# Spreading the high and low part steps of a pair over several attention steps on VectorE, and moving the sum of v away from the rows

## The chip, the cores and the metric

The kernel runs on one core of one Trainium2 chip. The metric is the device time of one execution in microseconds (us), as the median of several executions. Executions of one kernel scatter here by 0.3 to 1.4% (lowest to highest), so kernels are compared by runs taken in turn with the kernel before on the same chip.

Engines are named as in the profile: PE is TensorE (matmul), PEld its weight loads, DVE is VectorE, ACT is ScalarE, POOL is GpSimd, SP is SyncE, which here only issues DMA (SPq in the views is its queue). PSUM is the memory into which PE writes; an eviction is an instruction of another engine that reads a result out of it, and the program lets a PSUM tile be written again only when it has been read. "L200" is line 200 of the kernel; `hT<-g,f` means that tile hT is written from tiles g and f.

## The reference, cut to what matters

Attention with a mask by cluster, then a gated feed-forward network.

```python
B, H, S, D = 4, 8, 768, 64                     # 16 clusters per head
q_assign = argmax(q_n @ c_n.T);  k_assign = argmax(k_n @ c_n.T)   # normalised
mask = q_assign[..., :, None] == k_assign[..., None, :]
attn = softmax(where(mask, q @ k.T / 8, -1e9)) @ v
x = attn.transpose(0, 2, 1, 3).reshape(B * S, H * D)              # 3072 x 512
out = (sigmoid(x @ w_gate) * (x @ w_val)) @ w_out                 # d_ff 1536
```

## The kernel before

The kernel works in 16-bit floats. To keep the choice of cluster exact, every q and k value, scaled by 64, is split into a high part h (rounded to 16 bits) and a low part l (the remainder); h and l lie side by side, are transposed together, and go through the matmul as a contraction of 128. In the later batches a DMA does the transpose. The mask is added by "rows": one-hot vectors of the clusters, transposed, which are written over the low parts.

PE runs attention of one block of tokens and, interleaved piece by piece, the feed-forward network of the block before, first its input phase (`ffn_in`), then its output phase (`ffn_out`). A block of a later batch has 24 attention steps (4 head pairs x 6 key chunks) and a batch has 48 steps. A plan says in which step each side job is put into the program; the order of the program is the order of each engine's queue.

```python
natp = ctx.enter_context(tc.tile_pool(name="nat", bufs=8))
op_ = ctx.enter_context(tc.tile_pool(name="o", bufs=2))          # output tiles
fp_ = ctx.enter_context(tc.tile_pool(name="f", bufs=3, space=bass.MemoryType.PSUM))
avp = ctx.enter_context(tc.tile_pool(name="av", bufs=1, space=bass.MemoryType.PSUM))
...
def split_h(b, pr, side, eng=None):
    hl = HL[b, pr, side] = hlp.tile([128, 2 * NCH, 2, D], HP, name="hl")
    ...
    nc.vector.tensor_scalar(hl[:, :, 0, :], nat, SC, None, ALU.mult)          # L195
def split_l(b, pr, side):
    nc.vector.scalar_tensor_tensor(                                           # L200
        hl[:, :, 1, :], nat, SC, hl[:, :, 0, :], ALU.mult, ALU.subtract)
def split(b, pr, side, eng=None):
    split_h(b, pr, side, eng); split_l(b, pr, side)
...
def rows(b, pr):
    po = fp_.tile(...)                     # six PE transposes into it: L278
    nc.vector.tensor_scalar(ohc, po[:, 0:S], OHV, None, ALU.mult)             # L284
    ...                                    # four DMAs from SP: L287
def mean_v(b, hs):
    sp = fp_.tile([128, 512], FP, name="f")
    nc.tensor.matmul(out=sp[:, 0:n], lhsT=ones, rhs=VS[b][...], ...)          # L403
    nc.vector.tensor_scalar(SV[b][...], sp[:, 0:n], EPS, None, ALU.mult)      # L410
...
def ffn_in(b, c0, n):
    for fc in range(NFC):
        for i in range(2):                 # gate, value: 4 matmuls each, L531
            gv.append(fp_.tile([128, 512], FP, name="f"))
            ...
            nc.scalar.activation(g[:, 0:w], gv[0][:, 0:w], AF.Tanh, scale=0.5)  # L540
        nc.vector.scalar_tensor_tensor(hT[:, fc, 0:w], g, 1.0, gv[1], ...)      # L542
def ffn_out(b, c0, n):
    ...                                    # 12 matmuls of 512 columns, L552
        osb = op_.tile([128, DM], FP, name="osb")
        nc.scalar.activation(osb, o, AF.Copy, scale=0.5)                      # L561
        nc.sync.dma_start(out=dst[:, c0 + t, :], in_=osb)                     # L562
...
def by_dma(b, pr, load, a, base):          # pair pr of batch b; a is a step of batch base
    at(base, load, load_pair, b, pr)
    for i, side in enumerate((1, 0)):      # keys, then queries
        at(base, a + 0.5 * i, split, b, pr, side)
        at(base, a + 0.5 * i, trans_dma, b, pr, side)
        at(base, a + 9 + i, classify, b, pr, side)
    at(base, a + 11.5, rows, b, pr)
...
by_dma(1, 2, E + 23, E + 36, 0)            # E = 8
by_dma(1, 3, E + 33, E + 43, 0)
for b in range(2, B):
    for pr in range(NPR):
        by_dma(b, pr, 10 * pr, 8 + 10 * pr, b - 1)
```

The other lines that matter: L460 adds the matmul result of a pair (`avs<-av,sv`, DVE), L470 multiplies it on POOL (`x<-avs,ri`), L490 are the score matmuls, L499 the exponentials on ACT (`es`), L450 the matmuls with v (`av`), L75 the loads of q and k, L232 and L511 transposing DMAs.

The softmax here doesn't subtract the row's maximum and nothing guards it: scores larger than these inputs give would overflow.

## Time and profile before

| | before |
|---|---|
| median of 4 runs | 365.25 us (364.83 to 366.24) |
| span in the profile, granted clock | 363.4 us, 0.993 |
| PE / ACT / DVE busy | 344.6 / 244.6 / 169.5 us |

First the page of the kernel before: the span, the engines' busy time with its share of the span, and the shares of the chain of work that ended last.

```profile
span 363.4 us, 9364 instructions
...
PE 344.6 (95%) x3887; PEld 228.1 (63%) x3887; DVE 169.5 (47%) x374; ACT 244.6 (67%) x359; POOL 71.5 (20%) x105
...
PE 78%; DMA 6%; DVE 5%; issue 5%; ACT 4%; SPq 1%; POOL 0%; ACTq 0%; DVEq 0%
```

PE bounds the kernel, but busy time flatters it, because pipelined matmuls overlap in the record (one of 384 columns lasts about 0.32 us there, and the next starts after 0.162). So I use one measure throughout, worked out from the trace: the time between the starts of two consecutive matmuls, less the usual spacing after a matmul of that shape (162 ns for 384 columns, 215 for 512, 29 for 65, 25 for 16). I call the rest a *loss* and count those over 60 ns. An ordinary hand-over, as to or from the transposes of the rows, costs about 0.1 us. From 104 to 260 us the kernel before loses 8.8 us, and from 270 us to the end almost nothing.

What PE waited for, in the view of waits (us in total, times, longest):

```profile
PE f L403 <- DVE ohc L284: 1.7, 2, 1.0
PE f L278 <- ACT g L540: 1.5, 2, 0.8
PE sc L490 <- ACT es L499: 1.4, 3, 0.8
...
PE f L531 <- DVE hT L542: 1.3, 5, 0.4
...
PE av L450 <- DVE avs L460: 0.7, 3, 0.4
```

One such place in the timeline (start, duration, engine, line, what; in brackets the idle time before it and what ended it), the fourth pair of a batch:

```profile
156.57 0.55 DVE L195 TENSOR_SCALAR hl<-nat 128x768 f16<-128x768 f32 x1
...
157.15 0.96 DVE L200 SCALAR_TENSOR_TENSOR hl<-nat,hl 128x768 f16<-128x768 f32 x1
...
158.03 0.55 DVE L542 SCALAR_TENSOR_TENSOR hT<-g,f 128x384 f16<-128x384 f32 x1
...
158.49 0.72 DVE L195 TENSOR_SCALAR hl<-nat 128x768 f16<-128x768 f32 x1
...
158.63 0.49 PE L278 MATMUL f<-ident,ohw 128*64 128x128 f16 x6 [0.76 <-ACT g L540]
...
159.25 0.96 DVE L200 SCALAR_TENSOR_TENSOR hl<-nat,hl 128x768 f16<-128x768 f32 x1
...
160.12 0.54 DVE L284 TENSOR_SCALAR ohc<-f 64x768 f16<-64x768 f16 x1
...
160.72 0.28 PE L403 MATMUL f<-vs,ones 128*128 128x260 f16 x1 [0.67 <-DVE ohc L284]
```

DVE does h, l, an hT, h, l without a break; what comes behind them in its queue (hT, ohc) is late, and PE stands twice. (The first wait is put down to g of L540; that g and the late hT both end at 158.58.) In the view by windows (busy us of each engine in a stretch) the two stretches of this kind show it too:

```profile
150.00:166.00 16.00, 14.57 (x177) 9.72 (x176) 9.14 (x19) 10.49 (x16) 3.00 (x4) 1.00 0.65 171
...
232.00:248.00 16.00, 14.24 (x175) 9.53 (x174) 9.39 (x18) 10.16 (x15) 2.85 (x4) 1.00 0.71 168
```

The columns are PE, PEld, DVE, ACT and POOL, then the granted clock, the DMA share and GB/s. PE stands 1.4 and 1.8 us of 16, while DVE is busy for only 9 of them: not too much work, but work in one lump.

### The profile page before, as it was taken

The numbers are of one execution on the slowest core, as the hardware profiler recorded it, in microseconds if no ns is written. First come the engines' busy times: TensorE is split into PE (matmuls) and PEld (weight loads), VectorE is DVE, ScalarE is ACT, GpSimd is POOL, SyncE is SP. The second block draws the span as 40 slices with busy tenths as digits, with TensorE's granted clock in tenths as the row PEclk, the third lists the DMA queues.
The fourth block names the chain that finished last, engine by engine and source line by source line (L and its number), as shares of the span: only waits on it lengthen the run. The fifth ranks groups of instructions, "written<-read, shape, count | busy, mean of one in ns | idle before, by whom it ended". The sixth has DMA issues, their size and how long they took to land.

```text
span 363.4 us, 9364 instructions
## 1 busy us (share of the span) xinstructions
PE 344.6 (95%) x3887; PEld 228.1 (63%) x3887; DVE 169.5 (47%) x374; ACT 244.6 (67%) x359; POOL 71.5 (20%) x105
## 2 busy tenths in 40 slices
PE   8699999999989999989999999989999999999995
PEld 4597877876566656656556656656556656664652
DVE  4678686647164725373344725373313322331330
ACT  6687698686577575857577574857578867881421
POOL 3720021436010120425010120425000000000000
PEclk9989999999999999999999999999999999999999
DMA  8999279466629363760619373761310031003002
GB/s 258 338 203 191 66 223 185 128 142 89 154 95 248 71 168 89 200 160 12 164 67 261 30 199 86 236 112 27 73 74 2 0 74 58 2 2 101 32 0 87
DMA packets 67466, 42.72 MB, mean 118 GB/s; under 512 B 45568, under 2 KB 64352, under 8 KB 67424
## 3 DMA queue, kind: packets, MB, share of 16 engines
q1 hardware_dynamic: 61488, 37.38, 40.0%
q0 software_dynamic: 5792, 4.72, 8.3%
q8 instruction: 30, 0.49, 0.5%
q14 instruction: 12, 0.10, 0.1%
q10 hardware_dynamic: 144, 0.03, 0.0%
HBM read 28.61 MB, written 6.29 MB: 96 GB/s over the span
## 4 chain that ended last, share of the span: by engine, by line
PE 78%; DMA 6%; DVE 5%; issue 5%; ACT 4%; SPq 1%; POOL 0%; ACTq 0%; DVEq 0%
PE f L531 30%; PE f L552 16%; PE sc L490 15%; PE av L450 8%; PE f L243 4%; DMA vn<-in_v_dram 3%; ACT es L499 2%; PE f L216 2%; DVE hl L195 1%; DMA out_dram<-osb 1%; PE f L278 1%; DVE hT L542 1%; DMA nat<-in_q_dram 1%; DMA nat<-in_k_dram 1%; PE f L295 1%
## 5 line engine op out<-in xcount | busy, mean ns | idle before, releaser
L499 ACT ACTIVATE es<-sc,nbias 128x768 f16<-128x768 f32 (+1 forms) x200 | 173.6, 877 | 71.1 <-PE sc L490 66.2
L542 DVE SCALAR_TENSOR_TENSOR hT<-g,f 128x384 f16<-128x384 f32 (+1 forms) x96 | 51.1, 534 | 84.0 <-PE f L531 46.4
L450 PEld LDWEIGHTS <-es 128*128 128x128 f16 x1152 | 59.8, 97 | 27.1 <-issue 3.7
L470 POOL TENSOR_TENSOR x<-avs,ri 128x384 f16<-128x384 f32 (+1 forms) x32 | 26.8, 837 | 245.5 <-DVE ri L469 196.6
L450 PE MATMUL av<-va,es 128*128 128x65 f16 x1152 | 67.5, 194 | 1.3 <-DVE avs L460 0.7
L540 ACT ACTIVATE g<-f 128x384 f32<-128x384 f32 (+2 forms) x108 | 48.8, 452 | 18.6 <-PE f L531 9.7
L552 PE MATMUL f<-wo_194,hT 128*128 128x512 f16 x138 | 38.3, 379 | 0.0
L552 PE MATMUL f<-wo_193,hT 128*128 128x512 f16 x138 | 38.1, 379 | 0.0
L460 DVE TENSOR_TENSOR avs<-av,sv 128x390 f32<-128x390 f32 (+2 forms) x36 | 18.6, 516 | 41.0 <-PE av L450 40.4
L552 PEld LDWEIGHTS <-hT 128*128 128x128 f16 x276 | 24.4, 97 | 21.1
L200 DVE SCALAR_TENSOR_TENSOR hl<-nat,hl 128x768 f16<-128x768 f32 x32 | 32.6, 1017 | 0.8
L260 DVE TENSOR_REDUCE mx<-f 128x12 f32<-128x192 f32 x32 | 11.4, 356 | 32.3 <-PE f L243 32.2
L561 ACT ACTIVATE osb<-f 128x512 f32<-128x512 f32 x24 | 14.2, 593 | 17.6 <-PE f L552 15.3
L531 PE MATMUL f<-xT,w_186 128*128 128x384 f16 (+2 forms) x108 | 25.6, 308 | 0.0
L531 PE MATMUL f<-xT,w_187 128*128 128x384 f16 (+2 forms) x108 | 25.6, 307 | 0.0
L531 PE MATMUL f<-xT,w_188 128*128 128x384 f16 (+2 forms) x108 | 24.1, 307 | 0.4 <-DVE hT L542 0.4
L531 PE MATMUL f<-xT,w_191 128*128 128x384 f16 (+2 forms) x108 | 24.0, 307 | 0.5 <-ACT g L540 0.5
L531 PE MATMUL f<-xT,w_189 128*128 128x384 f16 (+2 forms) x108 | 23.8, 307 | 0.5 <-DVE hT L542 0.5
L531 PE MATMUL f<-xT,w_192 128*128 128x384 f16 (+2 forms) x108 | 23.6, 307 | 0.4 <-DVE hT L542 0.4
L531 PE MATMUL f<-xT,w_190 128*128 128x384 f16 (+2 forms) x108 | 23.8, 307 | 0.0
L531 PE MATMUL f<-xT,w_185 128*128 128x384 f16 (+2 forms) x108 | 23.6, 308 | 0.2
L370 POOL CAST va<-vn 128x768 f16<-128x768 f32 x15 | 14.2, 951 | 10.6 <-DMA vn<-in_v_dram 10.6
(221 smaller groups left out, 449.1 us busy)
## 6 DMA issues: line engine op xcount, KB each, us to landing
nat<-in_k_dram SPq DMA_DIRECT2D x16, 384.0 KB, 3.9
vn<-in_v_dram SPq DMA_DIRECT2D x8, 768.0 KB, 6.8
nat<-in_q_dram SPq DMA_DIRECT2D x16, 384.0 KB, 4.8
out_dram<-osb SPq DMA_DIRECT2D x24, 256.0 KB, 2.1
wo_193<-in_moe_w_out_dram POOLq DMA_DIRECT2D x1, 768.0 KB, 17.1
wo_194<-in_moe_w_out_dram POOLq DMA_DIRECT2D x1, 768.0 KB, 12.2
w_185<-in_moe_w_gate_dram POOLq DMA_DIRECT2D x1, 384.0 KB, 7.8
w_189<-in_moe_w_val_dram POOLq DMA_DIRECT2D x1, 384.0 KB, 8.0
```

Source lines behind the costliest of these rows:

```text
L200: nc.vector.scalar_tensor_tensor(hl[:, :, 1, :], nat, SC, hl[:, :, 0, :], ALU.mult, ALU.subtract)
L243: nc.tensor.matmul(out=cl[:, o : o + NCL], lhsT=T[b, pr, side][:, hh, bass.ts(c, 128)], rhs=cT[:, r, bass.ts(2 * pr + hh, NCL)], start=(r ...
L370: nc.gpsimd.tensor_copy(va[:, :, :, 0:D], src)
L450: nc.tensor.matmul(out=av[:, o : o + D + 1], lhsT=es[:, hh, bass.ts(g * n + t, 128)], rhs=VA[b, pr][:, hh, j0 + g, :], start=(j0 + g == 0 ...
L460: nc.vector.tensor_tensor(s[:, :, 0:n, :], av[:, 0 : 2 * n * (D + 1)].rearrange("p (h t d) -> p h t d", h=2, t=n), SV[b][:, 2 * pr : 2 * p ...
L470: (nc.vector if n == 1 else nc.gpsimd).tensor_tensor(x[:, 0:n, 2 * pr * D : 2 * (pr + 1) * D].rearrange("p t (h d) -> p h t d", h=2), s[:, ...
L490: nc.tensor.matmul(out=sc[:, hh, g * n * 128 : (g + 1) * n * 128], lhsT=T[b, pr, 1][0 : D + NCL, hh, bass.ts(j0 + g, 128)], rhs=rhs, start ...
L499: nc.scalar.activation(es[:, :, 0:w], sc[:, :, 0:w], AF.Exp, bias=nbias, scale=es_scale)
L531: nc.tensor.matmul(out=gv[i][:, 0:w], lhsT=wgv[i][fc * NQ // NFC][:, dc, bass.ts(fc % (NFC // NQ), 128)], rhs=xT[:, 0:n, dc, :], start=(dc ...
L540: nc.scalar.activation(g[:, 0:w], gv[0][:, 0:w], AF.Tanh, scale=0.5)
L542: nc.vector.scalar_tensor_tensor(hT[:, fc, 0:w], g[:, 0:w], 1.0, gv[1][:, 0:w], ALU.add, ALU.mult)
L552: nc.tensor.matmul(out=o, lhsT=hT[:, fc, bass.ts(t, 128)], rhs=wo[fc * 2 // NFC][:, fc % (NFC // 2), :], start=(fc == 0), stop=(fc == NFC ...
```

## The change

The intent is to break up that lump: h of the keys at step a, l at a+1, h of the queries at a+2, l at a+3. And the sum of v (mean_v) of the first four heads leaves the step next to the rows, which take a PSUM tile of the same pool.

```diff
     def by_dma(b, pr, load, a, base):
         at(base, load, load_pair, b, pr)
         for i, side in enumerate((1, 0)):
-            at(base, a + 0.5 * i, split, b, pr, side)
-            at(base, a + 0.5 * i, trans_dma, b, pr, side)
+            at(base, a + 2 * i, split_h, b, pr, side)
+            at(base, a + 2 * i + 1, split_l, b, pr, side)
+            at(base, a + 2 * i + 1, trans_dma, b, pr, side)
...
-        at(b - 1, e + 40, mean_v, b, range(0, H // 2))
+        at(b - 1, e + 44, mean_v, b, range(0, H // 2))
```

## The prediction

> **What bounds the kernel.** TensorE. The page gives PE 344.6 us of a 363.4 us span (95%), ACT 67%, DVE 47%. The Trainium skill ("Perfetto Trace Analysis", Identifying the Most-Contended Engine) warns that matmul busy time is a poor measure, so I compared starts of consecutive matmuls in the trace with their steady spacing (162 ns for 384 columns, 215 for 512, 29 for 65). From 90 us on PE issues back to back: stretches such as 130:140 or 210:220 lose 0.1 us in 10. What is lost, about 10 us between 90 and 330, comes in a few clusters, and nothing later makes it good.
>
> **Where they lie.** Every pair of a later batch puts h, l, h, l (L195 0.55 us, L200 0.96 us) on DVE within one attention step (about 1.4 us), so DVE is taken for 3.0 to 3.5 us, and the hidden-layer evictions (hT, L542) and sums (avs) queue behind. In the timeline and the waits: after the splits at 105.5/187.5 PE loses 0.68 us (ACT g, then hT); at 121.8/203.8 1.1 us (g, hT, avs); at 156.6/238.6 0.9 us, followed by 0.83/1.16 us where the matmul of mean_v (L403) waits for the eviction of the rows (ohc), issued half a step before it. At 76 to 87 us about 1.4 us (avs, hT). The splits at 140/222 fall in the output-projection phase and cost nothing. Sum: about 8.8 us, the most the change can win.
>
> **The change.** No instruction is added or removed. h and l of the keys go to steps a, a+1, of the queries to a+2, a+3; each transposing DMA follows its l. mean_v of the first four heads moves four steps later, away from the rows. In the input phase an hT falls due every 2.04 us or so (8 matmuls at 2.7 per half step). One l and one hT take 1.5 us, h, l and hT 2.06 us, so DVE keeps pace, and the three PSUM buffers hide the rest. Transposes start up to 3.5 us later, but are needed seven to nine steps later: no cost.
>
> **What stays.** The second pair's l at a+3 now meets POOL's casts of v, which follow its x product; L200 took 1.46 instead of 0.96 us in this trace each time such a POOL instruction ran beside it. That fits the Trainium skill ("SBUF — State Buffer", SBUF: two separate sides): the shared ports are an exclusive lock. There the two onehots, ohc and avs also fall among the four steps, so I expect about 0.5 us to stay per batch; about 0.3 at the fourth pair, and half of the loss before 90 us. The first pair's l leaves the x product and should be 0.96.
>
> **Estimate.** Recovered: 0.7 before 90 us; per batch 0.6 + 0.6 + 1.5, twice: about 6 us; less a discount for stalls that only move: 5.2 us. Predicted 360.2 us, 8 in 10 between 357.8 and 363.2. Faster by over 2% (below 358.1): 0.12; within 2%: 0.86; slower: 0.02.
>
> **What would show it.** PE's waits on hT, g and avs near those splits, and on ohc at L403, shrink to tenths; PE's busy sum unchanged, span shorter by the idle time. No 1.46 us L200 in the first pair, perhaps one in the second. DVE's busy sum the same. The last 100 us unchanged in length.
>
> **What would make it wrong.** The gaps are set by f-buffer rotation (classify, rows, mean_v each take one of three), so that single l steps still stall PE; mean_v, now behind the second sum_v in the program, waits for it; later transposes hold up loads or stores in SP's order; the part before 90 us is ordered by the framework and may fall out otherwise; the 1.3 us stall at 102 to 103 us (ACT waits for an output DMA) may grow or vanish.

## The result, and the profile after

Ratios here are the mean time of one kernel's fast runs over that of the kernel before's fast runs of the same rounds, so they are not quite the ratio of the medians.

| | before | after |
|---|---|---|
| median of 4 runs | 365.25 us | 360.81 us (360.29 to 362.46) |
| ratio | | 0.9882 (0.9843 to 0.9921) |
| span in the profile, granted clock | 363.4 us, 0.993 | 360.7 us, 0.975 |

The kernel gained 4.4 us, or 1.2%: inside the range, close to the 5.2 us forecast. The profiled run was the slowest of the four. First its page:

```profile
span 360.7 us, 9360 instructions
...
PE 346.0 (96%) x3887; PEld 230.2 (64%) x3887; DVE 170.2 (47%) x374; ACT 244.9 (68%) x359; POOL 73.8 (20%) x105
...
PE 85%; DMA 6%; ACT 3%; SPq 2%; issue 1%; DVE 1%; POOL 0%; ACTq 0%
```

DVE went from 5% to 1% of the chain. From the same matmul (the 601st of L531) to the end it is 89.1 us before and after: the last part kept its length, as predicted. The waits of PE after the change:

```profile
PE sc L490 <- ACT es L499: 2.2, 2, 2.0
...
PE f L531 <- ACT g L540: 0.5, 1, 0.5
...
PE av L450 <- DVE avs L460: 0.2, 1, 0.2
```

The waits on hT and ohc are gone, those on g and avs almost, but one wait on `es` has become 2.0 us long. First the place that was shown above, the fourth pair:

```profile
159.06 0.55 DVE L195 TENSOR_SCALAR hl<-nat 128x768 f16<-128x768 f32 x1
...
159.53 0.55 DVE L542 SCALAR_TENSOR_TENSOR hT<-g,f 128x384 f16<-128x384 f32 x1
...
160.00 1.11 DVE L200 SCALAR_TENSOR_TENSOR hl<-nat,hl 128x768 f16<-128x768 f32 x1
...
160.30 0.52 PE L278 MATMUL f<-ident,ohw 128*64 128x128 f16 x6
...
161.03 0.54 DVE L284 TENSOR_SCALAR ohc<-f 64x768 f16<-64x768 f16 x1
...
161.50 0.53 DVE L542 SCALAR_TENSOR_TENSOR hT<-g,f 128x384 f16<-128x384 f32 x1
...
161.96 0.54 DVE L195 TENSOR_SCALAR hl<-nat 128x768 f16<-128x768 f32 x1
```

Evictions now come between h and l of the keys and between the two sides, though nothing stands between h and l of the queries (161.96 and 162.54). PE has no wait in brackets. The windows over the same steps agree: PE is busy all the time.

```profile
152.00:168.00 16.00, 16.00 (x194) 10.75 (x191) 9.98 (x22) 12.07 (x18) 3.58 (x6) 1.00 0.71 144
...
230.00:246.00 16.00, 16.00 (x191) 10.79 (x190) 10.03 (x19) 12.02 (x19) 3.56 (x6) 1.00 0.58 141
```

By losses, 8.8 us between 104 and 260 us became 1.7 (all but a trifle of it ordinary hand-overs of 0.1 us), and 1.4 us between 76 and 90 us became 0.65. That is 7.8 us won. But part was given back at 102 us, where batch 1 begins. What SP issued there before, in the timeline of its queue:

```profile
93.69 1.46 SPq L511 DMA_TRANSPOSE xT<-x  x1
95.19 0.87 SPq L75 DMA_DIRECT2D nat<-in_k_dram  x1
96.51 0.38 SPq L75 DMA_DIRECT2D nat<-in_q_dram  x1
96.99 0.88 SPq L562 DMA_DIRECT2D out_dram<-osb  x2
```

And after:

```profile
90.24 1.41 SPq L232 DMA_TRANSPOSE T_2124<-hl  x1
...
94.55 1.52 SPq L511 DMA_TRANSPOSE xT<-x  x1
96.11 0.88 SPq L75 DMA_DIRECT2D nat<-in_k_dram  x1
97.04 0.48 SPq L75 DMA_DIRECT2D nat<-in_q_dram  x1
98.07 0.83 SPq L562 DMA_DIRECT2D out_dram<-osb  x2
```

The last pair's transpose of the queries, issued at 86.23 us before, comes at 90.24, and what stands behind it in SP's queue moves back: the first output store goes out at 98.07 in place of 96.99, although its tile was ready at about the same time (93.9 and 94.0). It landed at 103.2 (before 101.9). There are two output tiles, so the third output copy on ACT waits for it, the exponentials wait behind that copy, and PE waits for them. ACT and PE there before:

```profile
102.04 0.60 ACT L561 ACTIVATE osb<-f 128x512 f32<-128x512 f32 x1 [2.07 <-DMA out_dram<-osb]
...
103.48 0.48 PE L490 MATMUL sc<-T_1592,T_1555 80*128 80x384 f16 x2 [0.80 <-ACT es L499]
...
103.81 0.65 PE L531 MATMUL f<-xT,w_185 128*128 128x384 f16 x3
```

And after:

```profile
103.31 0.60 ACT L561 ACTIVATE osb<-f 128x512 f32<-128x512 f32 x1 [3.25 <-DMA out_dram<-osb]
...
104.75 0.80 PE L490 MATMUL sc<-T_1592,T_1555 80*128 80x384 f16 x2 [1.98 <-ACT es L499]
...
105.35 1.17 PE L531 MATMUL f<-xT,w_185 128*128 128x384 f16 x3
```

Three matmuls of 384 columns took 0.65 us in one and 1.17 us in the other. After its stand of 2 us PE ran at half rate, 320 ns from start to start in place of 162, from 105.0 to 110.8 us. By losses the stall went from 0.96 to 2.15 us and the half-rate stretch added 2.6: 3.7 us given back in this run. (7.8 less 3.7 is 4.1; the two profiled spans differ by 2.7, because the first 76 us lost 0.8 us more in this run, which varies from run to run by as much, and the rest is in gaps under 60 ns and hand-overs.)

### The profile page after: what moved, and what is told of

Same layout as the page of the kernel before. It is cut to its first block, busy times and chain, and to the rows that moved or that the text cites. A ratio compares the mean times of both kernels' runs of the same rounds, so it can differ in the third digit from the quotient of the medians.

```text
span 360.7 us, 9360 instructions
## 1 busy us (share of the span) xinstructions
PE 346.0 (96%) x3887; PEld 230.2 (64%) x3887; DVE 170.2 (47%) x374; ACT 244.9 (68%) x359; POOL 73.8 (20%) x105
## 4 chain that ended last, share of the span: by engine, by line
PE 85%; DMA 6%; ACT 3%; SPq 2%; issue 1%; DVE 1%; POOL 0%; ACTq 0%
PE f L531 34%; PE sc L490 16%; PE f L552 16%; PE av L450 9%; PE f L243 4%; DMA vn<-in_v_dram 3%; DMA nat<-in_k_dram 2%; PE f L278 2%; PE f L216 2%; ACT es L499 2%; DMA out_dram<-osb 1%; SPq L75 1%; PE f L295 1%; SPq L511 0%; DVE hl L200 0%
## 5 line engine op out<-in xcount | busy, mean ns | idle before, releaser
L470 POOL TENSOR_TENSOR x<-avs,ri 128x384 f16<-128x384 f32 (+1 forms) x32 | 28.0, 876 | 239.3 <-DVE ri L469 190.3
L200 DVE SCALAR_TENSOR_TENSOR hl<-nat,hl 128x768 f16<-128x768 f32 x32 | 31.4, 982 | 0.4
L531 PE MATMUL f<-xT,w_186 128*128 128x384 f16 (+2 forms) x108 | 25.6, 308 | 0.0
L531 PE MATMUL f<-xT,w_187 128*128 128x384 f16 (+2 forms) x108 | 25.6, 307 | 0.0
L531 PE MATMUL f<-xT,w_185 128*128 128x384 f16 (+2 forms) x108 | 24.9, 320 | 0.0
L531 PE MATMUL f<-xT,w_188 128*128 128x384 f16 (+2 forms) x108 | 24.1, 307 | 0.5 <-ACT g L540 0.5
L531 PE MATMUL f<-xT,w_189 128*128 128x384 f16 (+2 forms) x108 | 24.5, 315 | 0.0
L531 PE MATMUL f<-xT,w_191 128*128 128x384 f16 (+2 forms) x108 | 24.1, 308 | 0.0
L531 PE MATMUL f<-xT,w_190 128*128 128x384 f16 (+2 forms) x108 | 23.8, 307 | 0.0
L531 PE MATMUL f<-xT,w_192 128*128 128x384 f16 (+2 forms) x108 | 23.6, 308 | 0.0
```

The source lines that it names most:

```text
L200: nc.vector.scalar_tensor_tensor(hl[:, :, 1, :], nat, SC, hl[:, :, 0, :], ALU.mult, ALU.subtract)
L470: (nc.vector if n == 1 else nc.gpsimd).tensor_tensor(x[:, 0:n, 2 * pr * D : 2 * (pr + 1) * D].rearrange("p t (h d) -> p h t d", h=2), s[:, ...
L531: nc.tensor.matmul(out=gv[i][:, 0:w], lhsT=wgv[i][fc * NQ // NFC][:, dc, bass.ts(fc % (NFC // NQ), 128)], rhs=xT[:, 0:n, dc, :], start=(dc ...
```

## The experiments

Theory: (S) the spread of the splits carries the whole gain, and the wait at mean_v was part of the same DVE backlog; (O) the changed kernel gives a good part back through the output store. Rivals: (M) mean_v's move carries much of the gain; or the stall at 102 us was chance, or the low clock has nothing to do with it. All kernels gave correct results. Each was timed over 5 rounds (6 runs with the profiled one). The first four ran on one chip, beside a kernel before of 366.2 us median; the other eight in two calls on another chip, beside 366.24 and 365.95 us.

| label | median us | ratio to before (95%) |
|---|---|---|
| split_only | 358.67 | 0.9799 (0.9764 to 0.9834) |
| mean_only | 366.34 | 1.0010 (0.9965 to 1.0056) |
| after_o3 | 357.78 | 0.9763 (0.9727 to 0.9799) |
| before_o3 | 365.28 | 0.9979 (0.9943 to 1.0015) |
| after_again | 361.01 | 0.9840 (0.9789 to 0.9891) |
| split_only_o3 | 357.50 | 0.9755 (0.9719 to 0.9791) |
| two_steps | 360.17 | 0.9829 (0.9794 to 0.9864) |
| l_twice | 366.68 | 1.0011 (0.9963 to 1.0060) |
| after_load3 | 358.08 | 0.9775 (0.9736 to 0.9813) |
| mean_early_b1 | 359.45 | 0.9808 (0.9766 to 0.9849) |
| two_steps_o3 | 359.49 | 0.9815 (0.9779 to 0.9851) |
| split_o3_load3 | 358.01 | 0.9771 (0.9732 to 0.9811) |

### Each half of the change alone: split_only, mean_only

```diff
# split_only: the changed kernel with mean_v back
-        at(b - 1, e + 44, mean_v, b, range(0, H // 2))
+        at(b - 1, e + 40, mean_v, b, range(0, H // 2))
```

> The spread of the splits alone, mean_v left half a step after the rows. Theory S (the spread carries the gain, the stall at mean_v came from the DVE backlog of the splits): 361.0 to 361.8 us, the mean_v matmul L403 waits 0.1 to 0.5 us in place of 0.83 and 1.16. Rival M (most of the gain is mean_v's move): 363.0 us or more, L403 waits 0.8 us or more each time.

Measured: 0.9799, 358.67 us, which is even better than S expected. The matmul of mean_v (L403) has no wait in the later batches although it still follows the rows: at 157.5 and 236.2 us it starts without a loss. The first of the two, with no idle time in brackets:

```profile
157.49 0.29 PE L403 MATMUL f<-vs,ones 128*128 128x260 f16 x1
```

So the 0.83 and 1.16 us that PE lost there before were backlog of the splits. M is refuted.

```diff
# mean_only: the kernel before with mean_v moved
-        at(b - 1, e + 40, mean_v, b, range(0, H // 2))
+        at(b - 1, e + 44, mean_v, b, range(0, H // 2))
```

> mean_v moved alone, splits bunched as before. Theory S: 363.3 to 364.5 us, the waits on hT, g and avs after the splits (0.68, 1.1, 0.9 us) stay. Rival M: 361 us or less.

Measured: 1.001, no gain at all; both theories had expected some. The waits at the splits stayed, as S expected. The wait at L403 went, as M expected, but others came in its place. One line of its waits:

```profile
PE f L243 <- DVE sv L410: 1.3, 1, 1.3
```

In the first batch the moved mean_v falls among the splits of the last pair, its eviction (sv) queues behind them, and the next user of the PSUM tile loses 1.5 us at 87 us. In the later batches the next user of the rows' tile loses 0.5 and 0.16 us on ohc. With the splits bunched, moving one job only moves the stall.

### The output store: after_o3, before_o3, after_again, after_load3

```diff
# after_o3 and before_o3
-    op_ = ctx.enter_context(tc.tile_pool(name="o", bufs=2))
+    op_ = ctx.enter_context(tc.tile_pool(name="o", bufs=3))
```

> The changed kernel with three output tiles in place of two. Theory O (the changed kernel gives part of its gain back at 102 to 111 us: ACT waits 3.25 us for an output DMA, PE stands 2.1 us, and then runs at about half rate for 5 us at a granted clock of 0.76): the wait goes, the mean clock rises from 0.975 to 0.99 or more, 357.0 to 358.8 us. Rival (the late store has other causes and the wait moves elsewhere, or the low clock has nothing to do with the stall): 360 us or more.

Measured: 0.9763, 357.78 us. ACT's wait for the store is gone, and with it the half-rate stretch: in the window of 98 to 112 us PE is busy 13.87 us at a granted clock of 1.00, where the changed kernel had 11.88 at 0.76. First the kernel before, then the changed kernel, then this one:

```profile
98.00:112.00 14.00, 12.72 (x160) 8.36 (x158) 7.55 (x14) 9.43 (x14) 0.98 (x1) 1.00 0.55 150
```

```profile
98.00:112.00 14.00, 11.88 (x129) 7.32 (x126) 5.08 (x11) 6.82 (x10) 0.99 (x1) 0.76 0.36 118
```

```profile
98.00:112.00 14.00, 13.87 (x176) 9.28 (x175) 7.13 (x14) 11.05 (x15) 0.99 (x1) 1.00 0.64 181
```

The store itself was issued no sooner (98.5 us); only nobody waited for it. The mean clock of this profile rose to 0.986 only, short of the 0.99 expected (the other five runs: 0.990 to 0.995). From 10 to 24 us it has the same 0.63 as the changed kernel's profile, where the kernel before had 0.88; so the changed kernel's 0.975 is not all due to the stall at 102 us.

> The kernel before with three output tiles. Theory O: it has the same wait, 2.07 us at ACT and 1.26 us at PE, with no clock loss: 363.7 to 364.3 us. If it gains 3 us or more, the osb wait was as costly before and the change did not worsen it.

Measured: 0.9979. The median is 0.9 us below its neighbours', within the noise of these runs. So a third tile is worth little before the change and much after it. Between the two kernels with three tiles the change is worth 0.9763 / 0.9979 = 0.978, or some 7.9 us, in good agreement with the 7.8 us of losses won.

after_again is the changed kernel unedited, run in the same call as split_only_o3, two_steps and l_twice.

> The changed kernel unedited, so that it stands beside the others on one chip, and a second profile of the stall at 102 us. Theory O: the stall of ACT at the output DMA (over 2 us) is in this profile too, and the time is 1.5 to 3.5 us above the same kernel with three output tiles: ratio to before 0.983 to 0.990. If the stall in the first profile was chance, ratio 0.976 to 0.981.

Measured: 0.984, with the same stall in its profile: ACT waits 3.2 us for the store, PE loses 2.1 us and then runs at half rate for about 3 us. Its six runs went from 358.21 us (mean granted clock 0.993) to 363.03 (0.979): the scatter of this kernel is wider than that of its fully spread versions with three tiles (356.6 to 358.8). In the two profiles the half-rate stretch differs in length, 6 and 3 us; that this makes the scatter is likely, but not shown. The stall itself was not chance.

```diff
# after_load3: the changed kernel, loads of the first pair of the next batch at step 3
-            by_dma(b, pr, 10 * pr, 8 + 10 * pr, b - 1)
+            by_dma(b, pr, 10 * pr if pr else 3, 8 + 10 * pr, b - 1)
```

> The changed kernel with two output tiles, but the loads of q and k of the first pair of the next batch issued at step 3 in place of step 0 (so after the first output stores in SP's order). Theory O2 (the output store is late because SP issues it behind the transposes, the rows and these two loads of 384 KB, and it then lands behind them, 5.1 us where the median store takes 2.2): the first store of batch 1 is issued about 1.9 us sooner after the x transpose and lands in 2 to 3.5 us, the ACT wait of 3.2 us and the half-rate stretch go, ratio to before 0.974 to 0.979, as with three tiles. Rival (the store is late for another reason, as the transposing DMAs): the wait stays above 1.5 us, ratio 0.982 or more.

Measured: 0.9775, with two output tiles only. The timeline of this run:

```profile
94.39 1.52 SPq L511 DMA_TRANSPOSE xT<-x  x1
...
95.95 1.73 SPq L562 DMA_DIRECT2D out_dram<-osb  x2
...
97.74 0.45 SPq L75 DMA_DIRECT2D nat<-in_k_dram  x1
...
100.27 0.60 ACT L561 ACTIVATE osb<-f 128x512 f32<-128x512 f32 x1 [0.34 <-PE f L552]
```

The store is issued right behind the x transpose and landed at 98.8, in 2.9 us in place of 5.1; the third copy on ACT waits for PE, no longer for the store. Two edits that share nothing but the store give the same time, so the stall and the half-rate stretch come from the wait on it. What put the store late was SP's order. Moving the two loads in front of it was enough; that the transposes and rows, too, push it back is read from SP's timeline, and no run tests it alone.

### Does mean_v's move cost something: split_only_o3, mean_early_b1

split_only differed from the changed kernel by about 2 us, which S had not expected (358.67 and 361.01 us, on two chips; the intervals of the ratios overlap). split_only_o3 is split_only with the edit of after_o3.

> The spread alone with three output tiles. Theory P (mean_v's move is worth nothing by itself in the changed kernel; it differed from split_only only by the output wait): same as the changed kernel with three tiles, ratio to before 0.975 to 0.978. Rival Q (mean_v's move costs PE time of its own, about 2 us): ratio 0.970 to 0.973.

Measured: 0.9755, the same as after_o3 (0.9763). Without the output wait no worth of mean_v's place shows either way. The upper end of Q's band, 0.973, still lies inside the interval, but the profiles speak against Q too: from 76 to 260 us the version with the move (after_o3) loses 3.2 us, the one without it 4.0.

```diff
# mean_early_b1: only the mean_v that runs in the first batch goes back
-        at(b - 1, e + 44, mean_v, b, range(0, H // 2))
+        at(b - 1, e + (40 if b == 1 else 44), mean_v, b, range(0, H // 2))
```

> The changed kernel with mean_v of the second batch (the one prepared in the first) back at its old step, the other two left moved. Theory U (what mean_v's move costs in the changed kernel comes from its one move in the first batch, which pushes the output wait from 1.1 to 2.1 us of PE and into the low clock): ratio to before 0.977 to 0.982, as split_only; the output wait at ACT about 2.2 us and no half-rate stretch. Rival (the moves in the later batches cost, or the difference to split_only is noise of the runs): ratio 0.983 or more, or the half-rate stretch stays.

Measured: 0.9808, in the band of U, and its profile has ACT's wait at 2.1 us, a PE loss of 0.96 us and no half-rate stretch. But its runs (357.93 to 361.54 us) overlap with those of after_again, and so do the intervals. The profiles support that the one move in the first batch lengthens the output wait; the times do not settle it. Nor is it settled how: against split_only the changed kernel issues the store 0.6 us later (98.07 and 97.44), of which 0.5 us is PE being later too, and the store took 5.1 in place of 4.3 us to land. Why the landing differs stays open.

### How fine must the pieces be: two_steps, two_steps_o3, l_twice

```diff
# two_steps: h and l of a side in one step, the sides two steps apart
-            at(base, a + 2 * i, split_h, b, pr, side)
-            at(base, a + 2 * i + 1, split_l, b, pr, side)
-            at(base, a + 2 * i + 1, trans_dma, b, pr, side)
+            at(base, a + 2 * i, split, b, pr, side)
+            at(base, a + 2 * i, trans_dma, b, pr, side)
```

> The changed kernel with h and l of a side together in one step, the two sides two steps apart (blocks of 1.5 us on DVE in place of 3.0 to 3.5 or of 0.55 and 0.96). Theory R (an hT falls due every 2.04 us and DVE clears one block of 1.5 us plus an hT of 0.5 in that time, so only the bunch of four mattered): within 1 us of the changed kernel, waits on hT, g and avs under 0.3 us each. Rival T (each step needs its own short piece): waits of 0.3 to 0.6 us come back in the three input-phase clusters of each batch, 2 to 4 us slower than the changed kernel.

Measured: 0.9829, 360.17 us, by time the same as the changed kernel, as R said. But the waits are those of T: PE loses 0.92 us at the fourth pair in both batches, 0.3 at the second, 0.74 at 90 us. One line of its waits:

```profile
PE f L278 <- ACT g L540: 1.5, 2, 0.8
```

It lost these and saved elsewhere: its output wait cost PE only 0.91 us and left the clock alone. The comparison of times was spoiled by the other effect, so it was run again with three output tiles (the edit of after_o3).

> h and l of a side together, sides two steps apart, with three output tiles, so free of the output wait. Theory T (each step needs its own short piece): PE waits near the splits of 0.3 us at the second pair, 0.9 at the fourth, 0.7 at 90 us, as in two_steps; 1.5 to 3.5 us above the changed kernel with three tiles, ratio to before 0.981 to 0.986. Theory R: ratio 0.975 to 0.979.

Measured: 0.9815, 359.49 us, in the band of T. The waits stayed (0.92 twice, 0.3 twice, 0.72), and it is 1.5 to 2 us above the spread kernels without the output wait on the same chip (split_o3_load3, 358.01; split_only_o3, 357.50). So the separate steps for h and l are worth 1.5 to 2 us of the change's near 8; the larger part comes from parting the two sides.

```diff
# l_twice: the changed kernel, each spread l done twice
             at(base, a + 2 * i + 1, split_l, b, pr, side)
+            at(base, a + 2 * i + 1, split_l, b, pr, side)
```

> The changed kernel with every spread l step done twice (same result), 0.9 us more DVE work in 20 places. Theory R (slack of DVE in a step of about 1.4 us with the PSUM buffers behind it): blocks of 1.8 us exceed the slack a little where an hT falls due, 1 to 5 us slower than the changed kernel. If DVE time were on the chain outright: 12 to 18 us slower. If DVE had ample slack: under 0.5 us slower.

Measured: 366.68 us, 5.7 us above after_again in the same rounds, a little over the upper end expected. Added DVE work was 20 times 0.9, 18 us, so about a third came through. Most of it at 78 to 90 us, where PE loses 4.4 us against 0.65 in the changed kernel; in the input phases of the later batches stalls of 0.4 to 0.8 us come back. DVE has slack in a step, but less than one more l.

### A version that beats both: split_o3_load3

This one combines split_only with three output tiles and the later loads.

> The candidate that should beat both: splits spread, mean_v at its old step, three output tiles, the first pair's loads at step 3. If the output wait is fully gone with three tiles already, the later loads add nothing: ratio to before 0.973 to 0.977, same as split_only_o3 within noise. If loads ahead of the stores still cost something: 0.971 or less.

Measured: 0.9771. It adds nothing to either cure alone; there was one wait to cure. The versions without the output wait (split_only_o3, after_o3, after_load3, split_o3_load3) all lie at 357.5 to 358.1 us and cannot be told apart; all are about 3 us below the changed kernel and 8 below the kernel before.

## Why the prediction was right

The time fell inside the range, and close to the value, but two terms of the sum were off in opposite directions, so that it came so close is in part luck.

- *PE bounds the kernel, and the splits stall it through hT, g and avs.* Shown: the waits went with the bunching (after, split_only) and stayed with it (mean_only).
- *No instruction is added.* As predicted: matmul and DVE counts are equal, DVE is busy 170.2 us after 169.5.
- *Recovered: about 6 us.* Mis-sized: it was 7.8. The prediction left 0.5 us per batch at the second pair and 0.3 at the fourth; in the profile of after nothing but hand-overs was left there. In the seven other profiles of a kernel with the full spread and single l steps, 0.35 us was left at the fourth pair of the first of these batches (PE L278 waiting for hT), and in one of them 0.56 us at the second's.
- *The second pair's l meets POOL's casts.* They met, and it cost 0.15 us: L200 took 1.11 us at 129.24 (behind the x product) and at 208.33 (behind a cast), and the casts that came after took 1.5. "Each time" is too strong in the prediction: in the kernel before, L200 took 1.46 us at four such meetings after 76 us, but at 157.15 it had started first, took 0.96, and the cast took 1.36 in place of 0.83. The long L200 of the first pair (1.46) is 0.95, as predicted. The collisions moved rather than went, and POOL paid more: 73.8 us busy after 71.5. The page "SBUF — State Buffer" of the Trainium skill (SBUF: two separate sides) says that the second of two such instructions blocks until the first ends, and the trace agrees: an L195 ran 1.70 us in place of 0.55 (86.99 to 88.69) beside a POOL addition that ended at 88.26.
- *mean_v moves away from the rows, and the 0.83 and 1.16 us are recovered.* Right in sum, but the move is not what recovers them: those waits were the DVE backlog, and the spread alone removed them (split_only).
- *"A discount for stalls that only move": 0.8 us.* In proportion this is the term that was mis-sized most. The prediction named the stall at 102 us as one that "may grow or vanish", and said of the later transposes "no cost", though it listed SP's order among the risks. In the profiled run the stall grew by 1.2 us and brought 2.6 us of half rate with it. after_o3 and after_load3 show that the whole wait is worth about 3 us in the typical run. Some of it was there before the change (before_o3: 0.8 us, within the noise). What the change itself gave back is 2.1 to 3.6 us: 0.984 and 0.9882, the two ratios of the changed kernel, against 0.978 with three tiles.

So 7.8 us were won and 2 to 3.6 given back, which fits the measured 4.4 us (5.2 by the medians of after_again); the prediction had 6 and 0.8.

## What to carry to other kernels

Where the bounding engine is full and a helper engine is half idle, look for lumps in the helper's queue: here lumps of four instructions, 3 us together, cost PE 7.8 us over the run, and the same four, one per step between the evictions, cost almost nothing. When a job is moved later, follow every queue that it stands in: here the DMA that the job releases went later in an in-order issue queue, and a store behind it grew from a small stall into a large one. And judge an edit with such side effects away: with two output tiles a coarser spread looked as good as the fine one, with three it was 1.5 to 2 us worse.

## What the Trainium skill lacked or had wrong

- "TensorE: Matmul & The Clock Gate", What's actually happening, gives half rate, in its table of the two states, as the state after at least one idle window of about 3.4 us, and its rules for the kernel's author ask for no idle gaps over about 3 us. Here gaps of 2.0 to 2.15 us (after, after_again, l_twice) were each followed by 3 to 6 us at half rate (320 ns per matmul of 384 columns in place of 162, granted clock 0.76 over 14 us in after). Gaps of 0.9 to 1.1 us (before, split_only, two_steps, mean_early_b1) were not, nor gaps of 1.5 us (two in l_twice, one in mean_only). That the low rate is one half agrees with the page. Whether the gap alone or the thin work before it brought it on, no run here shows.
- "SBUF — State Buffer", SBUF: two separate sides, states the lock and gives a few measured examples, but none for steps like these: in the profile of after a 0.96 us DVE step of two SBUF inputs took up to 1.49 us, a 0.55 us step up to 1.70, and POOL instructions of 0.73 and 0.82 us up to 1.45 and 1.64.
- "Trainium Kernel Development and Optimization", Key Constraints, mentions the sequencer's issue time of DMAs and gives no figure in that section (figures for parts of it stand elsewhere in the skill). In the profile of after SP took 0.33 to 0.6 us for most loads and stores, and 1.3 to 1.5 us for 16 of 27 transposing DMAs, the others 2.1 to 2.8, in order, so that a store whose tile was ready at 94.0 us went out at 98.07. Where such a queue is crowded, the issue time is part of the wait.
